# A three-stage attention and expert kernel on one TensorE: the middle experts' last two forms by pairs of quarters, blocks' sums and remainders behind the additions, weight forms in other phases

## The chip, the core and the metric

The kernel runs on one core of a Trainium2 chip. The metric is device time in microseconds. Before the change it is 2186.79 us, the median of three runs (2185.93 to 2187.22). The core has a matrix engine (TensorE, PE in the profile), a vector engine (VectorE, DVE), a scalar engine (ScalarE, ACT), GpSimd (POOL) and a sync engine (SP) whose queue issues nearly all DMA transfers. Each engine works off its own list of instructions in the order in which the program gives them, and waits at an instruction until the semaphores it names are there.

## The reference

Attention over 4 batches, 8 heads, 1152 positions of width 64 (the queries pooled in pairs) gives 2304 tokens of width 512. They go through a mixture of 8 experts of which every one sees every token, and then through a soft mixture with 32 slots.

```
x = attention(q, k, v)                       # 2304 x 512
P = exp(x @ w_gate - max)                    # 8 rounds of row and column scaling
for e in range(8):
    h = maximum(x @ w1[e], 0)                # 512 x 1024
    out += P[:, e:e+1] * (h @ w2[e])         # 1024 x 512
return softmoe(out, phi, m2_w1, m2_w2)
```

The change is in the part of the experts, above all in experts 1 to 6.

## The kernel before

**Split operands.** All matrix work is done to nearly float32 precision in a faster type: an operand is held as a rounded half and the remainder. ScalarE writes the rounded half (a cast), VectorE subtracts it from the original (the remainder), and TensorE multiplies three pairs of halves into one sum. Weights go the same way, in tiles of 128 x 1024: `f_hi` is the cast (line 532), `f_lo` the remainder (line 535).

**Experts 1 to 6 by seven forms.** The first layer of an expert is not done as eight products of quarter matrices but as seven, of sums of quarters of the tokens and of the weights (the forms 11, 12, S2, S3, 22, S1, S4, numbered 0 to 6 in `PAIR`). The second layer is done in the same way by seven products (`PRODUCTS`) with weight forms 0 to 6. The sums of weights (`fsum`, line 507) are made one expert ahead on VectorE and stored to DRAM (`fstore`, line 512); later `stage_f` loads each form into one of four staging tiles, and `f_hi` and `f_lo` split it.

**Units, chunks, products.** The tokens are worked in three units per expert. `chunk(e, u, n, f)` (line 749) is form n for quarter f of the hidden half: six matmuls of 384 columns (line 763). `product(e, i, j)` (line 808) is product j of token block i: twelve matmuls of 256 columns (line 824), and then one VectorE instruction that adds the result into the accumulator (line 836). A unit has 28 chunks and 21 products (three blocks of seven), and the list says in which order they come:

- a first phase with forms 0 and 1: 8 chunks, 7 products (block 1 of the unit before),
- a middle phase with forms 2 to 4: 12 chunks, 7 products (block 2 of the unit before),
- the phase of additions, with forms 5 and 6: 8 chunks, 7 products (block 0 of this unit).

The unit's first phase accumulates in two PSUM tiles (`g`, pool of two). Form 0's sums are copied by ScalarE into four seed banks, and form 1 goes on in the same tile; the middle phase goes on in the seed banks. In the phase of additions form 5 of a quarter begins a `g` tile; VectorE adds it to a part of the hidden values (line 783, "the addition"), ScalarE applies the relu (line 769), and form 6 of the same quarter accumulates on in the same tile, so it waits for the addition; after it comes a second addition. The next quarter but one needs the tile free, so it waits for that second addition.

**What a block needs.** `second` says behind which item each step of a block is put: `h_split` (cast on ScalarE, line 734; remainder on VectorE, line 735) makes the operand of one product, and four VectorE sums (`h_sum`, line 728) come before four of them. The tiles `ho` are three, the accumulating tiles `y` two: a product waits for its remainder, and the first products of a block for the last accumulations of the block before.

**Order.** It is written out by hand. `item` appends a chunk or product to the list, `at(k, ...)` hangs a step behind item k, `run` (line 1210) reads strings of c (chunk) and p (product). In `FORMS` and `FORMS0` a row is the form's name, and the items, counted from the start of unit 2 of the expert before (or from the last block of expert 0), behind which it is staged, cast and subtracted; `jobs` place the loads of raw weight quarters and their sums, `where` the preparation of token sums in expert 0 (`prep`). Chunks of quarter 3 call `load_x(2)` (line 768): two operand tiles `xs` of five are loaded through SP's queue, behind all that was put there before.

Of the kernel before, what the change touches and what calls it, by code (L numbers as in the profile page):

```python
# [405 lines left out]
def tile_attention__moe__softmoe(ctx, tc, q, k, v, w_gate, w1, w2, phi, m2_w1, m2_w2, out):  # L406
    nc = tc.nc
    N, D = out.shape
    E = w_gate.shape[1]
# [162 lines left out]
    NU = NBLK // 3  # L572
# [622 lines left out]
    bounds, starts, base, slots = {}, {}, [], []  # L1195
# [25 lines left out]

    ZIG = lambda n: [(n, 0), (n, 1), (n + 1, 0), (n, 2), (n + 1, 1), (n, 3), (n + 1, 2), (n + 1, 3)]
    blocks = [[0, NBLK - 1, []]]
# [3 lines left out]
    for e in range(1, E - 1):  # L1227
        for u in range(NU):
            starts[e, u] = len(items)
            run(e, u, "ccppcpcpcpcpcpc", ZIG(0), todo)  # L1230
            run(e, u, "cpcpcpc" "cpccpc" "cpccpc", [(n, f) for n in (2, 3, 4) for f in range(4)], todo)
            bounds[e, u] = len(items) - 1
            new = [[e, 3 * u + i, []] for i in range(3)]
            blocks += new
            todo += new[:1]
            run(e, u, "ccpcpcpcpcpcpcp", ZIG(5), todo)
            todo += new[1:]
            plans.append((e, u, len(items) - 1))
# [6 lines left out]
    for n, (e, i, pos) in enumerate(blocks):  # L1245
        before = blocks[n - 1][2] if n else []
        if e == 0:
            b = pos[0] - 3
            second(e, i, pos, [b, b, b, b + 1, pos[0], pos[1], pos[2], pos[3], b + 1, pos[0]])
            continue  # L1250
        u, k = divmod(i, 3)
        end = bounds[e, u] + 15
        if k == 0:
            b = bounds[e, u]
            second(e, i, pos, [b - 4, b, b, b + 2, pos[0], pos[1], pos[2], pos[3], b + 3, b + 4])
        elif k == 1:
            second(e, i, pos, [end - 3, end - 1, end - 1, end, pos[0], pos[1], pos[2], pos[3], end, end + 1])
        else:
            second(e, i, pos, [before[4], before[4] + 1, before[5], before[6], pos[0], pos[1], pos[2], pos[3],
                               before[6], before[6] + 1])  # L1260

    late = dict(late=True)
    FORMS = (
# [3 lines left out]
    )  # L1267
    FORMS0 = (
# [3 lines left out]
    )  # L1272
    WS, VS = ("S3", "S1", "S2", "S4"), (3, 4, 2, 6)
    for e in range(E - 1):
        n = e + 1
        r = starts[e, 2] if e else base[8]
        if n < E - 1:
# [4 lines left out]
            if e:  # L1282
                jobs = ((starts[e, 1] - 7, starts[e, 1] - 1, 2), (starts[e, 1] + 12, starts[e, 1] + 22, 2))
            else:
                jobs = ((base[5] + 2, base[5] + 6, 2), (base[6] + 3, base[6] + 7, 2))
            for (s, d, w), raws, names, stage in zip(jobs, (W1Q, Q), (WS, VS), (stage_w, stage_v)):
# [4 lines left out]
        else:  # L1291
            at(r, (stage_p, n, 0), (stage_p, n, 4), **late)
            at(r + 14, (p_split, n, 0, "11"), **late)
            at(r + 36, (load_x7, 0), **late)
            at(r + 45, (load_x7, 1), **late)
            at(start7 + 14, (p_split, n, 4, "v0"), **late)

    where = [base[1] + 2, base[1] + 6, base[2] + 5, base[3] + 5, base[4] + 2, base[4] + 7, base[7] + 4, base[7] + 7, base[8]]
    for n, k in enumerate(where):
# [220 lines left out]
```

## Time and profile before

| | |
|---|---|
| median of three runs | 2186.79 us |
| the profiled execution | 2185.62 us, of which the span of the trace 2183.8 us |
| TensorE busy | 2070.2 us, 95% of the span; mean granted clock 0.982 |
| VectorE, ScalarE, GpSimd busy | 1440.4, 1008.6, 410.3 us |
| DMA | 367.42 MB, mean 168 GB/s |
| chain that ended last, by engine | PE 78%, DVE 11%, ACT 5%, DMA 3%, issue 2%, SP's queue 1% |

The profile is of one execution. Its time is 1.82 us above its span and 1.17 us below the median. TensorE's rows are pipelined: a row of six matmuls lasts a little longer than the distance to the next row's start. Idle time in brackets is that of the engine just before the row, with the line that released it. In what follows [rows n] are the groups of rows of the section after the next.

### The profile page before, as it was taken

The page shows a single profiled execution, that of the slowest core. Times are in us where ns is not written, and L with a number is a line of the kernel's source. Part 1 is how long each engine was busy: PE and PEld are TensorE (multiplying, and loading weights), DVE is VectorE, ACT ScalarE, POOL GpSimd, SP SyncE. Part 2 cuts the span into 40 slices and gives each one's busy share as a digit, 9 for nine tenths or more (in the row PEclk, how much of TensorE's full clock was granted, in tenths as well). Part 3 has the DMA queues.
Part 4 walks back from the last instruction along what each step waited for, and adds up shares of the span by engine and source line. Part 5 has one row for each costly group of instructions (what it writes and reads, how often), then busy time and mean ns, then how long its engine had stood idle before and what let it go on. Part 6 is the DMA issues. An engine that isn't in the chain of part 4 may idle for free.

```text
span 2183.8 us, 37987 instructions
## 1 busy us (share of the span) xinstructions
PE 2070.2 (95%) x14800; PEld 1883.5 (86%) x14800; DVE 1440.4 (66%) x2601; ACT 1008.6 (46%) x2110; POOL 410.3 (19%) x304
## 2 busy tenths in 40 slices
PE   8999999999999899989989998999999999999996
PEld 6777777778998889989989998999999999999863
DVE  6788778878677576766666667666766655644451
ACT  4666666665444534544454444445344534211232
POOL 6888888870000000000000000000000000000000
PEclk9999999999999999999999999999999999999997
DMA  7565555444365654455455445545544333577579
GB/s 181 141 142 126 136 129 127 99 123 156 136 239 200 216 190 138 152 178 175 157 172 204 136 144 179 191 141 185 186 150 144 115 105 103 182 272 249 205 242 285
DMA packets 198978, 367.42 MB, mean 168 GB/s; under 512 B 51472, under 2 KB 116304, under 8 KB 195792
## 3 DMA queue, kind: packets, MB, share of 16 engines
q1 hardware_dynamic: 196400, 363.53, 53.1%
q8 instruction: 117, 1.92, 0.4%
q10 hardware_dynamic: 2400, 1.47, 0.3%
q14 instruction: 61, 0.50, 0.1%
HBM read 276.38 MB, written 55.84 MB: 152 GB/s over the span
## 4 chain that ended last, share of the span: by engine, by line
PE 78%; DVE 11%; ACT 5%; DMA 3%; issue 2%; SPq 1%; ACTq 0%
PE y L824 23%; PE seed L763 10%; PE g L763 10%; PE o L271 6%; PE se L245 6%; PE S L216 4%; DVE ho L735 2%; DVE ht L728 2%; ACT ho L734 2%; DVE hr L783 1%; PE g L859 1%; PE g L860 1%; PE g L858 1%; PE y L881 1%; PE y L882 1%
## 5 line engine op out<-in xcount | busy, mean ns | idle before, releaser
L824 PE MATMUL y<-v,ho 128*128 128x256 f32 x5292 | 707.4, 285 | 20.3 <-DVE acc L836 14.0
L824 PEld LDWEIGHTS y<-v,ho 128*128 128x128 f32 x5292 | 687.4, 192 | 28.1 <-DVE acc L836 12.7
L763 PE MATMUL g<-xs,w 128*128 128x384 f32 x1728 | 354.8, 344 | 54.7 <-DVE hr L783 54.7
L763 PEld LDWEIGHTS g<-xs,w 128*128 128x128 f32 x1728 | 298.9, 193 | 63.8 <-DVE hr L783 63.0
L836 DVE SCALAR_TENSOR_TENSOR acc<-y,P,acc 128x256 f32<-128x256 f32 x378 | 182.1, 482 | 218.3 <-PE y L824 217.2
L256 POOL TENSOR_TENSOR acc<-acc,e 128x576 f32<-128x576 f32 x218 | 310.6, 1425 | 28.8 <-ACT e L248 15.1
L217 DVE TENSOR_REDUCE m<-S 128x1 f32<-128x384 f32 x432 | 227.8, 554 | 74.2 <-PE S L216 58.2
L985 POOL MEMSET HT<- 128x1024 f32 x2 | 1.9, 958 | 1406.1 <-PE y L824 1406.1
L735 DVE TENSOR_TENSOR ho<-hr,ho 128x512 fp32r<-128x512 f32 x252 | 174.0, 691 | 134.8 <-ACT ho L734 130.9
L248 ACT ACTIVATE e<-se 128x288 f32<-128x288 f32 x576 | 213.3, 411 | 95.2 <-PE se L245 94.2
L763 PE MATMUL seed<-xs,w 128*128 128x384 f32 x1296 | 249.3, 337 | 2.7 <-DMA xs<-xd0T 2.7
L763 PEld LDWEIGHTS seed<-xs,w 128*128 128x128 f32 x1296 | 222.6, 190 | 3.0 <-DMA xs<-xd0T 3.0
L734 ACT CAST ho<-hr 128x512 fp32r<-128x512 f32 x252 | 155.3, 617 | 103.8 <-PE y L824 95.6
L769 ACT ACTIVATE hr<-hr 128x384 f32<-128x384 f32 x144 | 75.0, 525 | 225.7 <-DVE hr L783 225.6
L734 ACT CAST ho<-ht 128x512 fp32r<-128x512 f32 x189 | 114.4, 619 | 130.5 <-PE y L824 73.3
L245 PE MATMUL se<-q,kd 128*128 128x288 f32 x576 | 166.6, 298 | 0.8 <-DVE kp L160 0.5
L245 PE MATMUL se<-qm,kd 128*128 128x288 f32 x576 | 164.7, 295 | 0.0
L735 DVE TENSOR_TENSOR ho<-ht,ho 128x512 fp32r<-128x512 f32 x189 | 129.6, 689 | 50.2 <-ACT ho L734 49.7
L271 PE MATMUL o<-e,vr 128*64 128x288 f32 x1152 | 160.9, 415 | 0.0
L216 PE MATMUL S<-kd,q 128*128 128x384 f32 x384 | 143.1, 375 | 2.3 <-DVE m L217 1.4
L271 PEld LDWEIGHTS o<-e,vr 128*64 128x64 f32 x1152 | 74.1, 136 | 50.4 <-issue 8.4
L216 PEld LDWEIGHTS S<-kd,q 128*128 128x128 f32 x384 | 72.7, 190 | 47.9 <-issue 21.3
(211 smaller groups left out, 3031.5 us busy)
## 6 DMA issues: line engine op xcount, KB each, us to landing
stg<-in_moe_w_dram SPq DMA_DIRECT2D x96, 512.0 KB, 5.9
w<-xd SPq DMA_DIRECT2D x72, 512.0 KB, 4.9
xs<-xd0T SPq DMA_DIRECT2D x48, 384.0 KB, 3.7
xs<-xd1T SPq DMA_DIRECT2D x48, 384.0 KB, 3.6
xs<-xd2T SPq DMA_DIRECT2D x48, 384.0 KB, 3.6
kd<-kp SPq DMA_DIRECT2D x31, 576.0 KB, 6.0
xs<-xd0B SPq DMA_DIRECT2D x36, 384.0 KB, 3.6
xs<-xd1B SPq DMA_DIRECT2D x36, 384.0 KB, 3.6
```

The lines of the kernel that those rows point to most:

```text
L216: nc.tensor.matmul(ps, lhsT=w, rhs=r[:, 384 * n:384 * n + 384], start=True, stop=True)
L217: nc.vector.tensor_reduce(out=M_[ph][:, x, n:n + 1], in_=ps, axis=AX.X, op=ALU.max)
L245: nc.tensor.matmul(ps, lhsT=kd[:, z, 128 * c:128 * c + 128], rhs=y[:, h, g], start=z == 0, stop=z == 1)
L248: nc.scalar.activation(out=e[:, g], in_=ps, func=AF.Exp, scale=1.0 / 16)
L256: nc.gpsimd.tensor_tensor(out=acc_[ph], in0=acc_[ph], in1=e, op=ALU.add)
L271: nc.tensor.matmul(O_[ph][64 * g:64 * g + 64, :288], lhsT=raws["v"][pi][:, h, c, :], rhs=E_[ph, c][:, g], start=c == 0, stop=c == 8,)
L734: nc.scalar.copy(o[:, 0], p)
L735: nc.vector.tensor_tensor(out=o[:, 1], in0=p, in1=o[:, 0].bitcast(F32), op=ALU.subtract)
L763: nc.tensor.matmul(ps, lhsT=w[:, a, kk, 128 * f:128 * f + 128], rhs=x[:, :, b], start=first and kk + z == 0, stop=kk == 1 and z == 2, skip ...
L769: relu = lambda o, b: nc.scalar.activation(out=o, in_=b, func=AF.Relu)
L824: nc.tensor.matmul(ps, lhsT=o[:, x, c], rhs=v[:, w, c], start=first and c + z == 0, stop=c + z == 5, skip_group_check=not first,)
L836: nc.vector.scalar_tensor_tensor(out=y, in0=ps, scalar=p, in1=y, op0=ALU.mult, op1=ALU.add)
```

## The change

The work is the same: every chunk, product, sum, split and transfer is there as often as before, and only the order changes.

```
-    ZIG = lambda n: [(n, 0), (n, 1), (n + 1, 0), (n, 2), (n + 1, 1), (n, 3), (n + 1, 2), (n + 1, 3)]
+    ORDER = lambda n: [(n + x, f + y) for f in (0, 2) for x in range(2) for y in range(2)]
...
-            run(e, u, "ccppcpcpcpcpcpc", ZIG(0), todo)
-            run(e, u, "cpcpcpc" "cpccpc" "cpccpc", [(n, f) for n in (2, 3, 4) for f in range(4)], todo)
+            run(e, u, "ccpccppccppcpcp", ORDER(0), todo)
+            run(e, u, "cpcpcpc" "cpcpcc" "cpcpcc", [(n, f) for n in (2, 3, 4) for f in range(4)], todo)
...
-            run(e, u, "ccpcpcpcpcpcpcp", ZIG(5), todo)
+            run(e, u, "pccpccpccppcpcp", ORDER(5), todo)
...
-        end = bounds[e, u] + 15
-        if k == 0:
-            b = bounds[e, u]
-            second(e, i, pos, [b - 4, b, b, b + 2, pos[0], pos[1], pos[2], pos[3], b + 3, b + 4])
-        elif k == 1:
-            second(e, i, pos, [end - 3, end - 1, end - 1, end, pos[0], pos[1], pos[2], pos[3], end, end + 1])
-        else:
-            second(e, i, pos, [before[4], before[4] + 1, before[5], before[6], pos[0], pos[1], pos[2], pos[3],
-                               before[6], before[6] + 1])
+        b, z = bounds[e, u], bounds[e, u] + 16
+        end = (e, u) == (E - 2, NU - 1)
+        second(e, i, pos, (
+            [b - 4, b, b + 1, b + 2, b + 5, b + 6, b + 7, b + 11, b + 3, b + 4],
+            [b + 12, z - 1, b + 14, z, z + 1, z + 2, z + 4, z + 5, z - 1, z + 1] if end else
+            [b + 12, b + 15, b + 14, b + 17, b + 19, b + 21, b + 22, b + 26, b + 16, b + 18],
+            [z + 6, z + 5, z + 7, z + 8, z + 9, z + 10, z + 12, z + 13, z + 6, z + 8] if end else
+            [z + 12, z + 10, z + 13, z + 14, z + 17, z + 19, z + 21, z + 24, z + 11, z + 16],
+        )[k])
...
-        (5, 72, 80, 82), (6, 74, 83, 85),
+        (5, 73, 79, 80), (6, 75, 82, 92),
...
-                jobs = ((starts[e, 1] - 7, starts[e, 1] - 1, 2), (starts[e, 1] + 12, starts[e, 1] + 22, 2))
+                jobs = ((starts[e, 1] - 3, starts[e, 1] + 1, 2), (starts[e, 1] + 12, starts[e, 1] + 20, 2))
...
-    where = [base[1] + 2, base[1] + 6, base[2] + 5, base[3] + 5, base[4] + 2, base[4] + 7, base[7] + 4, base[7] + 7, base[8]]
+    where = [base[1 + n // 2] + (2, 7)[n % 2] for n in range(9)]
```

The ten numbers given to `second` are the places of split 0, of the two sums s1 and s2, of splits 1 to 6, and of the sums s3 and s4. b is the last item of the middle phase, z the first of the next unit. All rows of `FORMS` and `FORMS0` get new places, of which one row is shown.

The first piece is TensorE's list in the phase of additions of unit 0 of expert 3, before: `g_13279`, `g_13290`, `g_13347` and `g_13404` are the tiles of quarters 0 to 3, `w_12788` is form 5, `w_12857` form 6; a chunk is two rows, and a `y` row is a product.

```order
L763 MATMUL g_13279<-xs_13126,w_12788 128x384 x3
L763 MATMUL g_13279<-xs_13198,w_12788 128x384 x3
L763 MATMUL g_13290<-xs_13126,w_12788 128x384 x3
L763 MATMUL g_13290<-xs_13198,w_12788 128x384 x3
L824 MATMUL y_13302<-v_13090,ho_13227 128x256 x12
L763 MATMUL g_13279<-xs_13200,w_12857 128x384 x3
L763 MATMUL g_13279<-xs_13266,w_12857 128x384 x3
L824 MATMUL y_13330<-v_13116,ho_13271 128x256 x12
L763 MATMUL g_13347<-xs_13126,w_12788 128x384 x3
L763 MATMUL g_13347<-xs_13198,w_12788 128x384 x3
```

And the same place now, where the quarters' tiles are `g_13295`, `g_13307`, `g_13370` and `g_13379`.

```order
L824 MATMUL y_13278<-v_13087,ho_13228 128x256 x12
L763 MATMUL g_13295<-xs_13123,w_12886 128x384 x3
L763 MATMUL g_13295<-xs_13199,w_12886 128x384 x3
L763 MATMUL g_13307<-xs_13123,w_12886 128x384 x3
L763 MATMUL g_13307<-xs_13199,w_12886 128x384 x3
L824 MATMUL y_13317<-v_13113,ho_13292 128x256 x12
L763 MATMUL g_13295<-xs_13201,w_12944 128x384 x3
L763 MATMUL g_13295<-xs_13267,w_12944 128x384 x3
L763 MATMUL g_13307<-xs_13201,w_12944 128x384 x3
L763 MATMUL g_13307<-xs_13267,w_12944 128x384 x3
L824 MATMUL y_13278<-v_13140,ho_13304 128x256 x12
L763 MATMUL g_13370<-xs_13123,w_12886 128x384 x3
```

A product now stands ahead of the first pair, form 6 of a quarter has one chunk and one product between it and form 5, and a new quarter begins one chunk and one product behind the form 6 that it waits for, where it was one product.

The second piece is VectorE's list at the same place, before: lines 728 are the block's sums, 735 remainders, 783 additions, 836 accumulations, and the two lines 535 are the remainders of weight forms 5 and 6 for the next block.

```order
L728 TENSOR_TENSOR ht_13276<-ht_13274,hr_12900 128x512
L535 TENSOR_TENSOR v_13245<-stg_13158,v_13245 128x1024
L783 TENSOR_TENSOR hr_13137<-g_13279,hr_13137 128x384
L783 TENSOR_TENSOR hr_13137<-g_13290,hr_13137 128x384
L735 TENSOR_TENSOR ho_13299<-ht_13276,ho_13299 128x512
L836 SCALAR_TENSOR_TENSOR acc0_9067<-y_13302,P_79,acc0_9067 128x256
L735 TENSOR_TENSOR ho_13316<-ht_13274,ho_13316 128x512
L728 TENSOR_TENSOR hr_12900<-hr_12900 128x4x128
L535 TENSOR_TENSOR v_13288<-stg_13177,v_13288 128x1024
L783 TENSOR_TENSOR hr_13045<-g_13279,hr_13045 128x384
```

And now, from the same product's accumulation on.

```order
L836 SCALAR_TENSOR_TENSOR acc0_9067<-y_13278,P_79,acc0_9067 128x256
L735 TENSOR_TENSOR ho_13292<-hr_13212,ho_13292 128x512
L783 TENSOR_TENSOR hr_13138<-g_13295,hr_13138 128x384
L735 TENSOR_TENSOR ho_13304<-ht_13274,ho_13304 128x512
L783 TENSOR_TENSOR hr_13138<-g_13307,hr_13138 128x384
L728 TENSOR_TENSOR hr_12874<-hr_12874 128x4x128
L836 SCALAR_TENSOR_TENSOR acc0_9067<-y_13317,P_79,acc0_9067 128x256
L728 TENSOR_TENSOR ht_13274<-hr_13212,ht_13274 128x512
L783 TENSOR_TENSOR hr_13044<-g_13295,hr_13044 128x384
L735 TENSOR_TENSOR ho_13340<-ht_13272,ho_13340 128x512
L783 TENSOR_TENSOR hr_13044<-g_13307,hr_13044 128x384
```

Both weight remainders have left this stretch (form 6's stands behind the fourth product's accumulation), and each remainder or sum stands behind an addition.

The third piece is SP's queue where unit 0 of expert 2 goes over into unit 1, before: lines 666 load operand tiles `xs`, lines 474 the four raw quarters.

```order
L666 DMA xs_11346<-xd1B11_7182 128x768
L474 DMA stg_11474<-in_moe_w1_dram 128x2x512
L474 DMA stg_11476<-in_moe_w1_dram 128x2x512
L474 DMA stg_11478<-in_moe_w1_dram 128x2x512
L474 DMA stg_11480<-in_moe_w1_dram 128x2x512
L666 DMA xs_11489<-xd1B11_7182 128x768
L666 DMA xs_11491<-xd1B21_7187 128x768
```

And now.

```order
L666 DMA xs_11466<-xd1B21_7202 128x768
L474 DMA stg_11524<-in_moe_w1_dram 128x2x512
L474 DMA stg_11526<-in_moe_w1_dram 128x2x512
L474 DMA stg_11528<-in_moe_w1_dram 128x2x512
L474 DMA stg_11530<-in_moe_w1_dram 128x2x512
L666 DMA xs_11538<-xd1B21_7202 128x768
L666 DMA xs_11540<-xd1T2_7322 128x768
```

The four quarters have moved behind the loads that follow form 5 and stand directly ahead of those that follow form 6.

## Rows read from the trace of the kernel before

**Rows 1.** The costliest groups: count | busy us, mean ns | idle before, releaser

```profile
L824 PE MATMUL y<-v,ho 128*128 128x256 f32 x5292 | 707.4, 285 | 20.3 <-DVE acc L836 14.0 <-ACT acc L832 5.3 <-DVE v L535 0.8
...
L763 PE MATMUL g<-xs,w 128*128 128x384 f32 x1728 | 354.8, 344 | 54.7 <-DVE hr L783 54.7
```

**Rows 2.** The chain of waits, one clean stretch: start us, us, what

```profile
1115.43 2.08 PE seed L763 x12
1117.51 1.43 PE y L824 x12
```

**Rows 3.** TensorE in time order: start us, us, engine, line, tiles, [idle before, releaser]

```profile
700.46 1.23 PE L763 MATMUL g<-xs,w 128*128 128x384 f32 x6
...
740.80 1.61 PE L763 MATMUL g<-xs,w 128*128 128x384 f32 x6 [0.53 <-DVE hr L783]
...
1135.42 1.33 PE L763 MATMUL g<-xs,w 128*128 128x384 f32 x6 [1.39 <-DVE hr L783]
...
1141.77 2.29 PE L763 MATMUL g<-xs,w 128*128 128x384 f32 x6 [3.60 <-DVE hr L783]
...
1164.99 1.70 PE L824 MATMUL y<-v,ho 128*128 128x256 f32 x12 [1.84 <-DVE acc L836]
...
1203.90 1.33 PE L763 MATMUL g<-xs,w 128*128 128x384 f32 x6 [0.25 <-DVE hr L783]
...
1208.23 1.31 PE L763 MATMUL g<-xs,w 128*128 128x384 f32 x6 [1.57 <-DVE hr L783]
...
1265.50 1.31 PE L763 MATMUL g<-xs,w 128*128 128x384 f32 x6 [0.25 <-DVE hr L783]
...
1269.82 1.31 PE L763 MATMUL g<-xs,w 128*128 128x384 f32 x6 [1.59 <-DVE hr L783]
...
1329.82 1.33 PE L763 MATMUL g<-xs,w 128*128 128x384 f32 x6 [1.39 <-DVE hr L783]
...
1843.99 1.31 PE L763 MATMUL g<-xs,w 128*128 128x384 f32 x6 [0.25 <-DVE hr L783]
```

**Rows 4.** ScalarE and VectorE at the start of a phase of additions, beside TensorE

```profile
1261.58 2.24 PE L763 MATMUL g<-xs,w 128*128 128x384 f32 x12
...
1261.78 0.49 ACT L769 ACTIVATE hr<-seed 128x384 f32<-128x384 f32 x1 [1.69 <-PE seed L763]
...
1262.30 0.62 ACT L734 CAST ho<-hr 128x512 fp32r<-128x512 f32 x1
...
1267.01 0.69 DVE L735 TENSOR_TENSOR ho<-ht,ho 128x512 fp32r<-128x512 f32 x1 [1.10 <-ACT ho L734]
...
1267.62 0.48 DVE L836 SCALAR_TENSOR_TENSOR acc<-y,P,acc 128x256 f32<-128x256 f32 x1
1268.01 0.68 DVE L735 TENSOR_TENSOR ho<-ht,ho 128x512 fp32r<-128x512 f32 x1
1268.61 0.68 DVE L728 TENSOR_TENSOR hr<-hr 128x512 f32<-128x512 f32 x1
1269.21 0.55 DVE L783 TENSOR_TENSOR hr<-g,hr 128x384 f32<-128x384 f32 x1
```

**Rows 5.** A weight form's remainder on VectorE in a phase of additions

```profile
1140.03 1.22 DVE L535 TENSOR_TENSOR v<-stg,v 128x1024 fp32r<-128x1024 f32 x1
```

**Rows 6.** Two windows: busy times of five engines, granted clock, DMA share, GB/s

```profile
1132.00:1134.00 2.00, 2.00 (x16) 1.83 (x14) 1.97 (x4) 0.00 (x0) 0.00 (x0) 1.00 1.03 390
...
1142.00:1144.00 2.00, 2.00 (x7) 2.00 (x8) 1.41 (x3) 0.79 (x2) 0.00 (x0) 0.50 0.73 210
```

**Rows 7.** TensorE's wait for an operand load in expert 1

```profile
731.27 5.50 PE L763 MATMUL seed<-xs,w 128*128 128x384 f32 x21 [2.67 <-DMA xs<-xd0T]
```

**Rows 8.** TensorE's wait in the last block of expert 0

```profile
676.00 2.93 PE L824 MATMUL y<-v,ho 128*128 128x256 f32 x12 [5.31 <-ACT acc L832]
```

**Rows 9.** Costliest groups: ScalarE's rounding of token sums in expert 0

```profile
L648 ACT CAST xt<-xs 128x512 fp32r<-128x512 f32 x18 | 11.2, 620 | 27.6 <-DVE xs L643 16.5 <-DMA xd2T<-xt 8.7 <-DVE w L535 2.4
```

**Rows 10.** SP's DMA queue where four weight quarters are loaded

```profile
1130.97 10.71 SPq L474 DMA_DIRECT2D stg<-in_moe_w_dram  x4
```

More of the change, by code (lines that the diff above doesn't have):

```diff
@@ L1245, in tile_attention__moe__softmoe @@
     for n, (e, i, pos) in enumerate(blocks):
-        before = blocks[n - 1][2] if n else []
         if e == 0:
@@ L1282, in tile_attention__moe__softmoe @@
             if e:
-                jobs = ((starts[e, 1] - 7, starts[e, 1] - 1, 2), (starts[e, 1] + 12, starts[e, 1] + 22, 2))
+                jobs = ((starts[e, 1] - 3, starts[e, 1] + 1, 2), (starts[e, 1] + 12, starts[e, 1] + 20, 2))
             else:
-                jobs = ((base[5] + 2, base[5] + 6, 2), (base[6] + 3, base[6] + 7, 2))
+                jobs = ((base[5] + 6, base[5] + 10, 2), (base[6] + 6, base[6] + 10, 2))
             for (s, d, w), raws, names, stage in zip(jobs, (W1Q, Q), (WS, VS), (stage_w, stage_v)):
@@ L1292, in tile_attention__moe__softmoe @@
             at(r, (stage_p, n, 0), (stage_p, n, 4), **late)
-            at(r + 14, (p_split, n, 0, "11"), **late)
+            at(r + 18, (p_split, n, 0, "11"), **late)
             at(r + 36, (load_x7, 0), **late)
```

10 rows, old and new, of tables (FORMS, FORMS0) are left out of this document.

## The prediction

> **What bounds the kernel now.** I read the shares of the engines first: TensorE is busy 95% of the span, so a change of order can give back only the rest, and what hangs on the clock. The costliest groups with their idle time come next [rows 1]: the chunks of line 763 waited 54.7 us for additions of line 783, the products of line 824 waited 20.3 us, of it 14.0 for VectorE's accumulations and 5.3 for one of ScalarE's. Then the chain of waits gives the clean pace, two chunks in 2.08 us and a product in 1.43 [rows 2]. A unit is 28 chunks and 21 products: 28 x 1.04 + 21 x 1.43 = 59.15 us. Last, TensorE in time order around the first form-6 chunk of each unit, a marker that recurs once a unit [rows 3]; the reader should see the stall before the marker in each unit, and compare distances of markers with 59.15.
>
> From 740.80 to 1843.99, 17 units, there are 1103.2 us instead of 17 x 59.15 = 1005.6: 97.6 lost. A unit without weight work, 1203.90 to 1265.50, takes 61.60, 2.45 too much; idle are 1.57 and 0.25, so each of two stalls costs 0.3 more than its idle time (the row before it runs out, two chunks taking 2.24 where starts are 2.08 apart [rows 2, 4], and the first chunk behind a stall has 1.31 or 1.33 against 1.23). An expert, 1135.42 to 1329.82, takes 194.4 instead of 177.5. Most of that is in its first unit: 3.60 idle before 1141.77, where a weight form's remainder of 1.22 [rows 5] stands ahead of the addition on VectorE, and 1.84 before a product at 1164.99. Behind the long stall the granted clock is 0.50, 1.2 of 2.4 GHz, after 1.00 ten microseconds earlier [rows 6], and the chunk there takes 2.29.
>
> The first unit, from 700.46 to 740.80, has 22 chunks and 8 products before its marker, 34.3 us, and took 40.3: 6.0 too much, 2.67 of them a wait for an operand load [rows 7]. The last unit has one more stall behind its marker, taken as 1.57 + 0.3 = 1.9. The middle experts thus lose 97.6 + 6.0 + 1.9 = 105.5. In expert 0 one product waits 5.31 for ScalarE and then lasts 2.93 instead of some 1.6 [rows 8]: with 0.3 that is 6.9. ScalarE was held there by its rounding of token sums, which waited 8.7 in all for earlier tiles to be stored [rows 9]. In sum 112.4 us could go.
>
> **The change part by part.** No instruction is added or removed, so nothing is charged for work. What counts is how much waiting stays.
>
> *The phase of additions.* Before, form 6 of quarter 0 had one product between it and form 5 of quarter 1, and the third quarter one product behind the form 6 whose tile it takes. Now a chunk and a product lie in each place. I set the new order against the clean pace, T being the start of the phase's first product: product 0 to 1.43, chunks (5,0), (5,1) to 3.51, product to 4.94, (6,0), (6,1) to 7.02, product to 8.45, (5,2) to 9.49, (5,3). On the other engines durations are from [rows 4], each instruction starting some 0.08 before the one ahead is over: relu 0.49, cast 0.62, remainder 0.68 (spacing 0.60), sum 0.68 (0.60), accumulation 0.48 (0.39), addition 0.55.
> - The relu of the middle phase starts 0.2 behind the next item's start, as 1261.78 stands to 1261.58. Cast of split 1 to 1.35, sums meanwhile to 2.1, the first accumulation, remainder 1 to 3.13: product 1 needs it at 3.51, 0.4 to spare.
> - Addition (5,0) 3.04 to 3.59, its relu to 4.14, cast 2 to 4.67, remainder 2 to 5.39, addition (5,1) 5.30 to 5.85; (6,1) wants it at 5.98, 0.1 to spare.
> - Sum, accumulation, sum; addition (6,0) 7.36 to 7.91, in time for (5,2) at 8.45. Its relu to 8.45, cast 3 to 8.98, remainder 3 9.01 to 9.70, and only behind it addition (6,1), 9.61 to 10.16. (5,3) takes that tile and wants it at 9.49. At 1269.82 a chunk started 0.06 after its addition's end, so it starts at 10.22: 0.72 late, with 0.12 for the slower first chunk 0.84.
> - From here each addition has at least 0.8 to spare, and the next unit's first product 0.3.
>
> So 0.84 a unit is left, 18 x 0.84 = 15.1. The price is from both sides: the 0.1 and 0.4 may fail as well, and the nearest row for a failing schedule is the cheapest unit of before, 2.45; or the 0.72 vanishes if ScalarE is quicker by one round. So 0 to 2.45, 0 to 44 over all units. I take the hand schedule, nearer to zero, since one wait and not two stands in it.
>
> *Weight forms.* Form 5's remainder leaves the phase; form 6's, 1.22 and a spacing of 1.14, now stands behind the fourth product's accumulation, in the first unit of an expert. There it puts the last remainder and the next unit's first accumulations back; of 1.14 some 0.7 is slack, so about 0.45 + 0.12 = 0.58 is left, 6 x 0.58 = 3.5 (0 if the slack is larger, 6 x 1.22 = 7.3 if there is none). The stall of 3.60, and with it the low clock of 1142 to 1144, goes: nothing of that length is left in which TensorE has nothing to do. The other forms go into the middle phase, where a unit's 12 chunks and 7 products leave VectorE with sums, remainders and accumulations and no additions.
>
> *Blocks 1 and 2.* Their sums and remainders now stand an item or two ahead of their products instead of in a row; the 1.84 before 1164.99 goes. In the middle phase the first remainder of a block is due within 0.1 of its product; I leave that at nothing, and it is in the range of the phase of additions.
>
> *SP's queue.* Four loads of raw quarters held SP for 10.71 us [rows 10], since each waits for a staging tile. They stood ahead of the loads behind form 5 and stand now ahead of those behind form 6. Staging tiles come free at about T + 11.6 to 15.4, the operand loads are called at T + 18 and used near T + 23. Four quarters are 2.1 MB; DMA moved 390 GB/s in a full window [rows 6], so 5.4 us. That ends before T + 23, and I leave 1 us in all. From the other side: all of 5.4 late at five transitions between experts, 27. Between 0 and 27 I take the value near zero, as the operand wait of before occurs once [rows 7].
>
> The Trainium skill, "DMA: Bandwidth & Descriptors", section "Anatomy of one DMA — SWDGE (gpsimd) path", says that a DMA's semaphore wait happens on the issuing sequencer before dispatch. The trace agrees as to SP: 10.71 us for four issues [rows 10]. By that rule a staging tile that comes free late delays every operand load behind it; by the row's times it does not reach the loads here. The rule gives the second rival below.
>
> *Expert 0 and the first unit.* Token sums are spread evenly over blocks 1 to 5, so ScalarE's rounding no longer waits in the last blocks: the 6.9 goes, but raw quarters now start behind the stores of token sums, and a form's sum may come later; I leave 1.5 (between 0 and 6.9). In the first unit I leave 1.9 of the 6.0 (three start-up matmuls of the seeds are in it; between 0 and 6.0).
>
> *Sum.* Left are 15.1 + 3.5 + 1.0 + 1.5 + 1.9 = 23.0, gone 112.4 - 23.0 = 89.4. The profiled execution took 2185.62, 1.82 of it outside the span of 2183.8, and was 1.17 below the median: 2185.62 - 89.4 + 1.17 = 2097.4, rounded 2097.
>
> **The rivals.** *Operand loads late.* Quarters wait for staging tiles, operand loads behind them: 5 x 5.4 = 27 instead of 1, 2123. For it speaks that SP was held 10.71 us and that an operand wait of 2.67 exists; against it that the quarters are called some 6 us ahead of the loads.
>
> *Additions stay exposed.* In each unit two stalls as in before's cheapest: 18 x 2.45 = 44 instead of 18.6, 2097 + 25.5 = 2122. For it: two places have 0.1 to spare or less by my schedule. Against it: what made the 1.57 was a tile wanted one product behind its form 6, now a chunk later.
>
> *Round trips on the path (the other side).* Remainders now stand between additions, and each waits for a relu, then a cast. At 1267.01 VectorE stood 1.10 for a cast [rows 4]. If each of five such trips in a phase reaches TensorE, 5 x (1.10 + 0.3) = 7.0 a unit, 126 instead of 18.6: 2097 + 107 = 2204, slower. It turns against the change once a unit loses more than 1.03 + 89.4 / 18 = 6.0. For it: the two engines are in series in five places of the new list. Against it: four of the five have a chunk and a product beside them, 2.47 us. The Trainium skill, "PSUM — Partial Sum Buffer", section "Engine vs sequencer instructions", says that ScalarE's and VectorE's queues are strictly first in, first out, so an early wait holds all behind it. The trace agrees at 1267.01, where 1.10 us of VectorE pass idle [rows 4].
>
> *The waits only move.* Every wait taken away returns elsewhere: 2187. Nothing in the profile demands it.
>
> **How the numbers follow.** Forecast 0.71 (2097); late loads 0.10 (2123); exposed additions 0.12 (2122); waits only move 0.03 (2187); round trips 0.04 (2204). The likeliest's own range is 2085 (if 12 of the 15.1 left in the phase of additions go too) to 2112 (a second wait of 0.84 in each unit, 15). The range that holds 8 in 10 goes to the loss of both middle rivals with some of the other terms: 2084 to 2132. A measurement of this kernel can tell 0.2%, 4.4 us, from no change. Faster by more than that 0.93, within it 0.03, slower 0.04.
>
> **What the profile after would show.** Right: the chunks of line 763 wait some 15 us and no longer 54.7 for line 783, one wait of about 0.7 before the chunk (5,3) of each unit; markers 60 us apart; no granted clock of 0.50 in the middle; the 5.31 before expert 0's last block gone; no wait on operand loads in the middle. Loads wrong: waits of several us of line 763 on `xs` behind the second unit's start. Additions wrong: two or more waits on line 783 in each unit. Round trips: products of line 824 idle for remainders of line 735. What would make the forecast wrong as a whole: a middle unit that stays above 61.6.

## The result, and the profile after

The changed kernel took 2100.47 us (median of four runs, 2096.87 to 2101.21), against 2186.92 for the kernel before (four runs). The ratio is 0.9602, with a 95% interval of 0.9586 to 0.9619. The forecast was 2097, range 2084 to 2132.

The profiled execution took 2101.21, with a span of 2099.0. In the groups by cost (columns as in [rows 1]) the waits of chunks for additions have fallen from 54.7 to 9.4, those of products from 20.3 to 6.1, and the operand wait [rows 7] is gone:

```profile
L824 PE MATMUL y<-v,ho 128*128 128x256 f32 x5292 | 691.9, 282 | 6.1 <-DVE ho L735 3.4 <-ACT acc L832 1.0 <-DVE acc L836 0.9
L763 PE MATMUL g<-xs,w 128*128 128x384 f32 x1728 | 337.2, 337 | 10.5 <-DVE hr L783 9.4 <-ACT seed L771 0.8 <-DMA xs<-xd1B 0.3
...
L763 PE MATMUL seed<-xs,w 128*128 128x384 f32 x1296 | 247.6, 335 | 0.0
```

To see where the time came from, cut TensorE's time at three starts: the first row of line 794 (expert 0 begins), of line 763 (expert 1), of line 858 (expert 7). First the kernel before, in time order, whose row of line 763 at 700.46 is in [rows 3]:

```profile
483.97 0.28 PE L794 MATMUL g<-xs,w 128*128 128x256 f32 x1
...
1860.80 0.28 PE L858 MATMUL g<-w 128*128 128x256 f32 x1
```

And the changed kernel:

```profile
485.63 0.28 PE L794 MATMUL g<-xs,w 128*128 128x256 f32 x1
...
699.55 1.23 PE L763 MATMUL g<-xs,w 128*128 128x384 f32 x6
...
1775.76 0.28 PE L858 MATMUL g<-w 128*128 128x256 f32 x1
```

Cut in the same way, all profiles give this table (us; what follows expert 1 to 6 is expert 7 and the soft mixture):

| kernel | attention | expert 0 | experts 1 to 6 | what follows | span | median |
|---|---|---|---|---|---|---|
| before | 483.97 | 216.49 | 1160.34 | 323.0 | 2183.8 | 2186.92 |
| changed | 485.63 | 213.92 | 1076.21 | 323.2 | 2099.0 | 2100.47 |
| changed, once more | 483.08 | 214.18 | 1075.96 | 323.1 | 2096.3 | 2098.57 |
| remainder 3 moved | 482.90 | 213.59 | 1062.12 | 323.2 | 2081.8 | 2085.04 |
| raw quarters of expert 0 moved | 483.49 | 210.01 | 1076.99 | 323.8 | 2094.3 | 2093.75 |
| both | 483.05 | 209.87 | 1060.60 | 322.6 | 2076.1 | 2079.25 |
| old order of additions | 483.19 | 214.22 | 1127.43 | 323.5 | 2148.3 | 2149.10 |
| new order alone | 483.38 | 216.44 | 1126.42 | 322.6 | 2148.8 | 2150.51 |
| old places of sums and remainders | 484.49 | 214.36 | 1103.57 | 322.9 | 2125.3 | 2127.04 |
| old weight forms | 483.11 | 215.42 | 1093.31 | 322.9 | 2114.7 | 2115.93 |
| old expert 0 | 482.84 | 216.62 | 1083.35 | 322.5 | 2105.3 | 2107.55 |
| old raw loads | 483.49 | 214.36 | 1080.54 | 323.2 | 2101.6 | 2103.01 |

Experts 1 to 6 gave 84.1 us, expert 0 gave 2.6; attention, whose code is the same, took 1.7 more in this execution and 0.9 less in the next. The stretch of experts 1 to 6 as one window of each profile, before and then now (the stretch and its length, busy us of TensorE, of its weight loads, of VectorE, ScalarE and GpSimd, granted clock, DMA share, GB/s):

```profile
700.46:1860.80 1160.34, 1089.29 (x7481) 1076.83 (x7479) 761.32 (x1236) 538.52 (x965) 0.00 (x0) 0.98 0.48 159
699.55:1775.76 1076.21, 1064.80 (x7481) 1055.90 (x7479) 747.89 (x1236) 526.87 (x964) 0.00 (x0) 1.00 0.52 172
```

TensorE's idle time there fell from 71.0 to 11.4, which is 59.6 of the 84.1. The other 24.5 is its busy time, with the same matmuls: rows that stretch around a wait, and rows under a lower clock. In windows of 2 us the granted clock is below 0.97 in 29 of them before and in none now.

A middle unit now has one wait on TensorE, before the chunk (5,3), and the same one each time. These are TensorE's rows of the changed kernel with idle time over 0.15 between 900 and 1300 (those between that are like the others are left out; columns as in [rows 3]):

```profile
938.11 1.83 PE L763 MATMUL g<-xs,w 128*128 128x384 f32 x9 [0.25 <-DMA xs<-xd1B]
...
1105.49 1.31 PE L763 MATMUL g<-xs,w 128*128 128x384 f32 x6 [0.51 <-DVE hr L783]
1165.67 1.32 PE L763 MATMUL g<-xs,w 128*128 128x384 f32 x6 [0.51 <-DVE hr L783]
...
1285.88 1.32 PE L763 MATMUL g<-xs,w 128*128 128x384 f32 x6 [0.51 <-DVE hr L783]
```

The distance is 60.10 us, against 61.60 in before's cheapest unit and the forecast's 59.15 without waits. From the first to the second unit of an expert it is longer: 60.18 in expert 3 (1105.49 to 1165.67), 60.17 and 60.13 in experts 4 and 5, but 60.63 in expert 2, with the wait of 0.25 for operands in it, and 60.78 in expert 1, with a wait of 0.45 for an accumulation. The wait of 0.51 before 1285.88 followed back, ScalarE:

```profile
1283.60 0.52 ACT L769 ACTIVATE hr<-hr 128x384 f32<-128x384 f32 x1 [1.53 <-DVE hr L783]
1284.04 0.60 ACT L734 CAST ho<-ht 128x512 fp32r<-128x512 f32 x1
```

VectorE in the same stretch:

```profile
1283.02 0.55 DVE L783 TENSOR_TENSOR hr<-g,hr 128x384 f32<-128x384 f32 x1
1284.67 0.69 DVE L735 TENSOR_TENSOR ho<-ht,ho 128x512 fp32r<-128x512 f32 x1 [1.10 <-ACT ho L734]
1285.28 0.55 DVE L783 TENSOR_TENSOR hr<-g,hr 128x384 f32<-128x384 f32 x1
```

The addition of (6,0) at 1283.02 releases a relu, the relu is ahead of the cast of split 3, the cast releases the remainder at 1284.67, and only behind that stands the addition of (6,1), 1285.28. It ends at 1285.83, and the chunk starts at 1285.88. VectorE itself was idle for 1.10 us ahead of that.

In expert 0 the 5.31 of [rows 8] is gone, but four smaller waits are there. TensorE:

```profile
618.98 1.70 PE L824 MATMUL y<-v,ho 128*128 128x256 f32 x12 [0.98 <-ACT acc L832]
...
637.67 1.46 PE L824 MATMUL y<-v,ho 128*128 128x256 f32 x10 [1.92 <-DVE ho L735]
...
660.79 1.45 PE L824 MATMUL y<-v,ho 128*128 128x256 f32 x10 [0.94 <-DVE ho L735]
665.70 3.11 PE L824 MATMUL y<-v,ho 128*128 128x256 f32 x24 [0.46 <-DVE acc L836]
```

VectorE ahead of the 1.92 stood at the sum of a weight form (line 507) that waited for a raw quarter, with the block's remainders behind it:

```profile
635.78 1.22 DVE L507 TENSOR_TENSOR stg<-stg 128x1024 f32<-128x1024 f32 x1 [2.91 <-DMA stg<-in_moe_w_dram]
636.93 1.29 DVE L735 TENSOR_TENSOR ho<-ht,ho 128x512 fp32r<-128x512 f32 x2
```

And SP's queue, where the raw quarters (line 474) stand behind stores of token sums and of operands:

```profile
603.24 18.77 SPq L651 DMA_DIRECT2D xd2T<-xt  x8
622.06 0.63 SPq L614 DMA_DIRECT2D xd<-w  x1
622.74 5.50 SPq L624 DMA_DIRECT2D xd2B<-w  x8
628.28 2.01 SPq L474 DMA_DIRECT2D stg<-in_moe_w_dram  x4
```

### The profile page after: what moved, and what is told of

Its sections match the earlier page's. It is cut to its first block, busy times and chain, and to the rows that moved or that the text cites. A ratio compares the mean times of both kernels' runs of the same rounds, so it can differ in the third digit from the quotient of the medians.

```text
span 2099.0 us, 38009 instructions
## 1 busy us (share of the span) xinstructions
PE 2046.2 (97%) x14800; PEld 1861.9 (89%) x14800; DVE 1426.4 (68%) x2601; ACT 997.5 (48%) x2110; POOL 410.4 (20%) x304
## 3 DMA queue, kind: packets, MB, share of 16 engines
q8 instruction: 117, 1.92, 0.4%
## 4 chain that ended last, share of the span: by engine, by line
PE 80%; DVE 9%; ACT 4%; DMA 3%; issue 2%; SPq 1%; POOL 0%; ACTq 0%; DVEq 0%; POOLq 0%
PE y L824 24%; PE seed L763 10%; PE g L763 9%; PE o L271 7%; PE se L245 7%; PE S L216 4%; DVE ht L728 2%; DVE hr L783 2%; PE g L859 2%; PE g L860 2%; PE g L858 2%; PE y L881 1%; PE y L882 1%; PE y L883 1%; ACT hr L769 1%
## 5 line engine op out<-in xcount | busy, mean ns | idle before, releaser
L824 PE MATMUL y<-v,ho 128*128 128x256 f32 x5292 | 691.9, 282 | 6.1 <-DVE ho L735 3.4
L824 PEld LDWEIGHTS y<-v,ho 128*128 128x128 f32 x5292 | 673.7, 190 | 11.6 <-issue 4.7
L763 PE MATMUL g<-xs,w 128*128 128x384 f32 x1728 | 337.2, 337 | 10.5 <-DVE hr L783 9.4
L763 PEld LDWEIGHTS g<-xs,w 128*128 128x128 f32 x1728 | 292.3, 189 | 19.0 <-DVE hr L783 15.5
L778 ACT COPY hr<-seed 128x384 f32<-128x384 f32 x144 | 69.2, 480 | 127.9 <-PE seed L763 127.4
```

The lines of the kernel that those rows point to most:

```text
L763: nc.tensor.matmul(ps, lhsT=w[:, a, kk, 128 * f:128 * f + 128], rhs=x[:, :, b], start=first and kk + z == 0, stop=kk == 1 and z == 2, skip ...
L824: nc.tensor.matmul(ps, lhsT=o[:, x, c], rhs=v[:, w, c], start=first and c + z == 0, stop=c + z == 5, skip_group_check=not first,)
```

## The experiments

All are compared with the kernel before on the same chip; for the size of an effect the table's columns are used, since attention moves by up to 2.8 us from run to run. The medians of the table come from four sets of runs, in which the kernel before took 2186.92, 2183.05, 2182.80 and 2183.80; the changed kernel was in the first two of them.

**The changed kernel once more.**

> The changed kernel once more, as the yardstick for the others on the same chip. Theory (the middle is regular, what varies from run to run lies ahead of the experts): 2100.5 within 2, and the distance of the markers, the form-6 or form-5 chunks that wait for line 783, stays 60.10 within 0.05. Rival (the middle varies): markers move by some tenths from unit to unit.

2098.57 us, ratio 0.9614 (0.9601 to 0.9627). From the second unit on the markers stand 60.08 to 60.21 apart, and 60.76 behind the first, so the theory's 0.05 does not hold for the first unit of an expert. Experts 1 to 6 take 1075.96, 0.25 less than the first time, and the wait for operands in expert 2 is not there: the middle is regular up to such tenths, and what varies more lies ahead of it.

**Remainder 3 behind the second addition.**

```diff
-            [b - 4, b, b + 1, b + 2, b + 5, b + 6, b + 7, b + 11, b + 3, b + 4],
+            [b - 4, b, b + 1, b + 2, b + 6, b + 6, b + 7, b + 11, b + 3, b + 4],
```

> One number moved: the remainder of split 3 stands behind the second addition of form 6 and no longer ahead of it. Theory: this remainder, which waits for a relu and a cast, is what holds addition (6,1) and so the chunk (5,3), 0.51 idle and some 0.3 of restart in each unit; gone, 18 x 0.8 = 14 us less than the changed kernel, 2086, units of 59.3. Rival 1: the wait moves to the product that needs this remainder, units stay at 60.1, 2100. Rival 2: the addition is late because of ScalarE's relu of (6,0), which is not moved: 2100 and the wait still names line 783.

2085.04 us, ratio 0.9550 (0.9537 to 0.9563). Experts 1 to 6 took 1062.12, 14.0 less than the mean of the two profiles of the changed kernel. TensorE at the place of the wait, chunks (5,2) and (5,3) now in one row, two in 2.09:

```profile
1272.25 1.59 PE L824 MATMUL y<-v,ho 128*128 128x256 f32 x12
1273.68 2.25 PE L763 MATMUL g<-xs,w 128*128 128x384 f32 x12
1275.77 3.03 PE L824 MATMUL y<-v,ho 128*128 128x256 f32 x24
...
1335.07 3.03 PE L824 MATMUL y<-v,ho 128*128 128x256 f32 x24
```

The wait did not move to the product that needs the remainder (both rows of products run without idle time). The last two rows are the same place in two units that follow each other, 59.30 apart. So the wait cost 60.10 - 59.30 = 0.80 a unit, and its cause is shown: the remainder's place in VectorE's list, not ScalarE's relu, which was not moved. The 0.15 by which 59.30 is above 59.15 is not the wait's.

**Raw quarters of expert 0.**

```diff
-                jobs = ((base[5] + 6, base[5] + 10, 2), (base[6] + 6, base[6] + 10, 2))
+                jobs = ((base[5] + 4, base[5] + 10, 2), (base[6] + 6, base[6] + 12, 2))
```

> In expert 0 the four raw quarters of the first layer are called two items earlier, ahead of the operand stores of block 6, and the sums of those of the second layer two items later. Theory: the three waits of products for remainders and accumulations in expert 0 (1.92, 0.94 and 0.46 at 637.67, 660.79 and 665.70) come from VectorE standing at a weight sum whose raw quarters had not landed (2.91 and 0.79 idle); they shrink, 2 to 4 us less than the changed kernel, 2097 to 2098. Rival: the quarters wait for staging tiles, not behind the stores: 2100.

2093.75 us, ratio 0.9593 (0.9580 to 0.9606). Expert 0 took 210.01, 4.0 less, at the upper end of what was expected; of its waits only the first, for ScalarE's accumulation, is left, and VectorE's waits of 2.91 and 0.79 for raw quarters are gone. The quarters now go ahead of the nine stores of operands (lines 614 and 624), but still behind the eight stores of token sums (line 651), which take 19.05 of SP's queue. The median is 4.8 below the changed kernel's on this chip. Which of the two places gave how much was not tried apart.

**Both.** The two edits above in one kernel.

> The two edits together (remainder 3 behind the second addition, raw quarters of expert 0 as in the run before this). Theory: they lie in different stages and add up, 14 + 3 = 17 less than the changed kernel, 2083 to 2084. Rival: one of the two gives nothing, 2086 or 2097.

2079.25 us, ratio 0.9524 (0.9511 to 0.9537): 19.3 below the changed kernel on this chip. The parts, 13.5 and 4.8 in the medians, add up to 18.3; the theory had put expert 0's part at 3, and its time is some 4 above the measured one. This version beats both kernels.

**The old order in the phase of additions**, all else new.

```diff
-            run(e, u, "pccpccpccppcpcp", ORDER(5), todo)
+            run(e, u, "ccpcpcpcpcpcpcp", ZIG(5), todo)
```

> The changed kernel, but the phase of additions in the order of before (quarters in zigzag, one product between the two forms of a quarter); sums, remainders and weight forms stay in their new places. Theory: the order of the chunks is what spares the additions; the cheapest unit of before lost 2.45 and one of the changed kernel 0.95, so at least 18 x 1.5 = 27 comes back, 2126, more (to 2150) where new remainders stand ahead of additions with little room. Rival (the places of sums and remainders carried the gain): within 5 of the changed kernel, 2100.

2149.10 us, ratio 0.9845 (0.9830 to 0.9859): experts 1 to 6 51 more than in the changed kernel, the upper end. In every unit but the first TensorE waits 2.04, longer than before's 1.57 in a plain unit, one without weight work [rows 3], since the new place of the remainder meets an order without room. Besides, at the start of the second unit of experts 1 to 5 a chunk waits 0.99 to 1.40 for operand tiles, 6.2 us in all, which neither theory nor rival had. TensorE, such a wait of 2.04 and then one for operands:

```profile
1115.88 1.58 PE L824 MATMUL y<-v,ho 128*128 128x256 f32 x12
1119.50 1.31 PE L763 MATMUL g<-xs,w 128*128 128x384 f32 x6 [2.04 <-DVE hr L783]
...
1137.84 1.83 PE L763 MATMUL g<-xs,w 128*128 128x384 f32 x9 [1.08 <-DMA xs<-xd1B]
```

VectorE, where behind the remainder an accumulation and a sum too come ahead of the addition at 1118.90:

```profile
1117.30 0.69 DVE L735 TENSOR_TENSOR ho<-ht,ho 128x512 fp32r<-128x512 f32 x1 [1.10 <-ACT ho L734]
1117.90 0.48 DVE L836 SCALAR_TENSOR_TENSOR acc<-y,P,acc 128x256 f32<-128x256 f32 x1
1118.30 0.68 DVE L728 TENSOR_TENSOR hr<-hr 128x512 f32<-128x512 f32 x1
1118.90 0.55 DVE L783 TENSOR_TENSOR hr<-g,hr 128x384 f32<-128x384 f32 x1
```

**The new order alone**, on the kernel before.

```diff
-            run(e, u, "ccppcpcpcpcpcpc", ZIG(0), todo)
-            run(e, u, "cpcpcpc" "cpccpc" "cpccpc", [(n, f) for n in (2, 3, 4) for f in range(4)], todo)
+            run(e, u, "ccpccppccppcpcp", ORDER(0), todo)
+            run(e, u, "cpcpcpc" "cpcpcc" "cpcpcc", [(n, f) for n in (2, 3, 4) for f in range(4)], todo)
...
-            run(e, u, "ccpcpcpcpcpcpcp", ZIG(5), todo)
+            run(e, u, "pccpccpccppcpcp", ORDER(5), todo)
```

> The kernel before, with TensorE's new order of chunks and products alone; sums, remainders, weight forms and expert 0 as before. Theory: the waits behind VectorE's additions in plain units go (27), those from weight forms and from rows of sums and remainders stay in part: 2140 to 2160. Rival 1 (the order is everything): 2105, expert 0's 3 left out. Rival 2 (the order alone is worth nothing, as the old remainders now stand in new places ahead of additions): 2175 or more.

2150.51 us, ratio 0.9850 (0.9835 to 0.9864): 33.9 of the 84.1 us in experts 1 to 6. The number is the theory's, and both rivals fall, but the theory's mechanism does not hold. The waits of plain units have not gone, they stand at other chunks. TensorE, the second form-6 chunk of two units and a chunk between:

```profile
1186.66 1.32 PE L763 MATMUL g<-xs,w 128*128 128x384 f32 x6 [0.93 <-DVE hr L783]
1189.78 2.35 PE L763 MATMUL g<-xs,w 128*128 128x384 f32 x12 [0.36 <-DVE hr L783]
...
1248.22 1.33 PE L763 MATMUL g<-xs,w 128*128 128x384 f32 x6 [0.94 <-DVE hr L783]
```

From the first of these rows to the last are 61.56 us, against before's 61.60. What the order alone gave lies where weight forms are: from the phase of additions of unit 0 to that of unit 1 of expert 4 it takes 65.4, where before's marker distance was 68.5, and from unit 2 of expert 3 to unit 0 of expert 4 61.7, where it was 64.3. The longest wait for an addition there is 1.06 and no longer 3.60.

**The old places of sums and remainders**, with the new order, weight forms and expert 0. The three rules that the diff removes stand again in place of the lists; one line of it:

```diff
-            [b - 4, b, b + 1, b + 2, b + 5, b + 6, b + 7, b + 11, b + 3, b + 4],
+            second(e, i, pos, [b - 4, b, b, b + 2, pos[0], pos[1], pos[2], pos[3], b + 3, b + 4])
```

> The changed kernel, but sums and remainders of each block by the rules of before; TensorE's order, weight forms and expert 0 stay new. If the parts add up, the order alone (middle experts 1126.4 us) less the weight forms (17.2 in the run that put them back) less expert 0's part in the first unit (7.1) leaves 1102, 26 more than the changed kernel's 1076.2: 2126. Theory: additions again stand behind sums and remainders, two or more waits for line 783 in each plain unit, 20 to 30 more. Rival (with the new order the places of sums and remainders hardly matter, and order plus forms explain all): within 5 of the changed kernel, 2100 to 2105.

2127.04 us, ratio 0.9740 (0.9724 to 0.9756). Experts 1 to 6 took 1103.57; 1102 had been worked out from three other runs. There are two waits in a plain unit again, which takes 61.59. TensorE:

```profile
1172.53 1.31 PE L763 MATMUL g<-xs,w 128*128 128x384 f32 x6 [0.94 <-DVE hr L783]
1175.66 2.35 PE L763 MATMUL g<-xs,w 128*128 128x384 f32 x12 [0.39 <-DVE hr L783]
```

**The old weight forms**, the table `FORMS` of before for experts 2 to 6.

```diff
-        (5, 73, 79, 80), (6, 75, 82, 92),
+        (5, 72, 80, 82), (6, 74, 83, 85),
```

(one line of it; the whole table goes back.)

> The changed kernel, but the weight forms of experts 2 to 6 staged, cast and subtracted where they were before. Theory: a form's remainder of 1.22 in the phase of additions, where the schedule has 0.1 to 0.8 of room, stops TensorE again, in the first unit of five experts and with the low clock behind it: of the 17 that an expert of before lost, some 9.6 are not the plain units' 3 x 2.45; I expect 3 to 10 an expert, 2115 to 2150. Rival (the new order has room enough): within 3 of the changed kernel.

2115.93 us, ratio 0.9690 (0.9674 to 0.9706), at the low end of the theory: 17.2 in experts 1 to 6, 3.4 for each of five experts. Markers put 1.1 of the 3.4 in the third unit of the expert before and 2.3 in the first unit, where the theory had it all. In both a form's remainder stands again between two additions. VectorE, third and first unit:

```profile
1047.42 1.22 DVE L535 TENSOR_TENSOR w<-stg,w 128x1024 fp32r<-128x1024 f32 x1
...
1106.53 1.22 DVE L535 TENSOR_TENSOR v<-stg,v 128x1024 fp32r<-128x1024 f32 x1
...
1108.67 0.55 DVE L783 TENSOR_TENSOR hr<-g,hr 128x384 f32<-128x384 f32 x1
```

And TensorE, which in the third unit waits 1.67 where it was 0.51, and in the first for that addition and for the next:

```profile
1049.16 1.33 PE L763 MATMUL g<-xs,w 128*128 128x384 f32 x6 [1.67 <-DVE hr L783]
...
1109.27 1.31 PE L763 MATMUL g<-xs,w 128*128 128x384 f32 x6 [0.44 <-DVE hr L783]
1111.53 1.31 PE L763 MATMUL g<-xs,w 128*128 128x384 f32 x6 [0.95 <-DVE hr L783]
```

The granted clock stays at 1.00 there, so the low clock of [rows 6], which I had expected back, is no part of the 17.2.

**The old expert 0**: `FORMS0`, `where` and the raw loads of expert 0 as before.

```diff
-    where = [base[1 + n // 2] + (2, 7)[n % 2] for n in range(9)]
+    where = [base[1] + 2, base[1] + 6, base[2] + 5, base[3] + 5, base[4] + 2, base[4] + 7, base[7] + 4, base[7] + 7, base[8]]
```

(`FORMS0` and one line of `jobs` go back too.)

> The changed kernel, but token sums, raw quarters and weight forms in expert 0 as before. Theory: the 5.31 wait for ScalarE's accumulation in the last block comes back and the three smaller waits go; the stage of expert 0 was 216.5 us before and 213.9 in the changed kernel, so 2.6 more, 2103. Rival (the prediction's term): 5.4 more, 2106.

2107.55 us, ratio 0.9654 (0.9640 to 0.9668): 7 more than the changed kernel's first median, which is from another set of runs, and above both numbers. Expert 0 took 2.6 more, as the theory said, but both theories had left out what is behind it: 7.3 in experts 1 to 6, in their first unit. TensorE there:

```profile
730.44 5.45 PE L763 MATMUL seed<-xs,w 128*128 128x384 f32 x21 [2.74 <-DMA xs<-xd0T]
...
743.06 1.33 PE L763 MATMUL g<-xs,w 128*128 128x384 f32 x6 [0.94 <-DVE hr L783]
...
749.65 1.31 PE L763 MATMUL g<-xs,w 128*128 128x384 f32 x6 [2.08 <-DVE hr L783]
```

The operand wait of [rows 7] is back, and so are waits for additions: remainders of weight forms (line 535) start on VectorE at 739.06, just ahead of the first addition, and at 743.53 and 747.91, between additions; in the changed kernel none stands between the first addition and the chunk (5,3).

**The old raw loads** in experts 1 to 5.

```diff
-                jobs = ((starts[e, 1] - 3, starts[e, 1] + 1, 2), (starts[e, 1] + 12, starts[e, 1] + 20, 2))
+                jobs = ((starts[e, 1] - 7, starts[e, 1] - 1, 2), (starts[e, 1] + 12, starts[e, 1] + 22, 2))
```

> The changed kernel, but in experts 1 to 5 the raw quarters for the next expert are called four items earlier, ahead of the operand loads behind form 5, and the sums two items earlier or later, as before. Theory: the four quarters still find staging tiles when the operand loads are not yet due, so between 0 and 2 us an expert, 2100 to 2108. Rival (the prediction's second rival): operand loads stand 5.4 us behind the quarters at five transitions, 27 more, 2127, with waits of line 763 for operand tiles.

2103.01 us, ratio 0.9633 (0.9619 to 0.9648). The rival falls: chunks of experts 1 to 6 wait 0.7 us for operand tiles in all. The 4.5 in experts 1 to 6 are mostly of another kind, which neither theory named: VectorE's sums of weight forms come two items earlier, ahead of accumulations that products wait for. Such waits grew from 0.45 to 3.56. Loads and sums were not moved back apart. TensorE in the second unit of experts 1 and 3 (in 4 and 5 as in 3):

```profile
760.18 1.67 PE L824 MATMUL y<-v,ho 128*128 128x256 f32 x12 [1.60 <-DVE acc L836]
...
1122.53 1.67 PE L824 MATMUL y<-v,ho 128*128 128x256 f32 x12 [0.65 <-DVE acc L836]
```

## Why the prediction was right, point by point

**The whole.** The case given 0.71 came, 3.5 us above its number, which is inside its own range of 2085 to 2112. On the profiled execution 2096.2 was forecast and 2101.21 measured, 5.0 more: 1.7 in attention, which is the same code, 2.8 in expert 0, 0.2 in what follows, 0.4 outside the span; experts 1 to 6 took some 0.1 less than forecast.

**Experts 1 to 6.** Forecast were 105.5 lost before and 21.5 left; without waits they would take 1160.34 - 105.5 = 1054.8, so 21.4 are left. That they agree so well is in part luck: the terms are off by a few us each, in both directions. *The phase of additions* was right in place and order: one wait, before (5,3), caused by the remainder that I had named, and its removal took the wait away. Its price, 0.84, is near the 0.80 that the removal gave, but by two errors that offset each other: idle was 0.51 where I had 0.72, and around it 0.29 is lost where I had 0.12 ((5,2) to (5,3) is 1.71 and (5,3) to the next product 1.17, each instead of 1.04). My 59.15 for a unit without waits was 0.15 too low, as 59.30 with the remainder moved shows: 18 x 0.15 = 2.7 of the 105.5 could not go. *The weight form's* 0.58 in the first unit measured 0.03 to 0.08 in experts 3 to 5; why is not shown, but it fits more slack than the 0.7 that I set against its 1.14. *SP's queue* left a wait of 0.25 in one profile and none in the next, where I had 1. The T + 11.6 to 15.4 for its raw quarters stood there without rows; in the unit with T = 1275.65 SP was held by them from 1287.65 for 3.85, T + 12.0 to 15.9. The wait of 0.45 in expert 1, behind a sum of weight forms, I had not named. *The first unit* left more than 1.9: from 699.55 to its chunk (5,3) at 743.69 lie 25 chunks and 10 products, 40.3 us, and it took 44.1, of which 0.7 is the unit's own wait, so 3.1. *The clock* I had not priced apart; it is in the distances that I summed, and as forecast no granted clock of 0.50 is left there.

**Expert 0** is the term that was most mis-sized. I left 1.5 of 6.9; 216.49 - 213.92 = 2.6 went and 4.3 stayed. The mechanism was named (raw quarters behind the stores of token sums, a form's sum late), but not that VectorE would stand at that sum with the block's remainders behind it. Moving the raw quarters ahead, with later sums of the second layer, gave 4.0 back. On the other hand the same edits are worth 7.3 in the first unit, where I had credited 4.1: 9.8 measured for this piece against 9.5 in the sum.

**The rivals.** *Operand loads late* was wrong for this kernel: its own chunks wait 0.25 for operand tiles. It is no empty rival, though: with the old order of additions, and the raw loads in their new places, its sign is there, waits of line 763 on `xs` in the second unit of five experts, but at some 1.2 each and not 5.4. *Additions exposed*: one wait a unit, not two; with the old places of sums and remainders it would have been right (two waits a unit, 27.5 us more in experts 1 to 6, where I had priced it at 25.5). *Round trips*: VectorE does stand 1.10 us for a cast several times in each phase of additions, as at 1284.67, but only one of them reached TensorE; the others have a chunk and a product beside them. *The waits only move* did not happen.

**How the parts combine.** Undone one at a time, they cost in expert 0 and experts 1 to 6 together 51.5 (order of additions), 27.8 (sums and remainders), 18.6 (weight forms, of which 1.4 in expert 0, that the edit does not touch), 9.8 (expert 0), 4.8 (raw loads): 112.5, where all together gave 86.7. They do not add up: an order with room for additions is of use when nothing long stands ahead of them, and the other way round. A plain unit shows it best. It takes 61.60 before, 61.6 with the new order and the old places of sums and remainders, 62.1 to 63.1 with the old order and the new places, and 60.10 with both. The new order alone gave 34, none of it in plain units. Why undoing the order costs more than that is seen in the rows of that run: the new remainders, without the room, make a wait of 2.04 where before's was 1.57, operand tiles come late, and behind some of the waits the granted clock falls, so that of its 51 us in experts 1 to 6 idle time is 35.7 and longer rows are 15.7. One more place moved with the change, a split of expert 7's operands (`p_split`); no run undid it apart, and what follows expert 6 stays within 322.5 to 323.8 in all of them.

## What to carry to other kernels

When two engines that work in series (here relu and cast on one, addition and remainder on the other) feed a third, write the third's list so that between an item and the one that needs its result there is enough unrelated work to cover the feeders' chain, and in the feeders' lists put what the third waits for ahead of what has a later due time. Here one product, 1.43 us, was too little; a chunk and a product, 2.47 us, were enough in all places but one. Both lists have to change together: either one alone gained nothing in a plain unit. A schedule made by hand from start distances in the trace found the one wait that was left, and its removal was one number. A sum that waits for a load does harm through what is queued behind it: look whether its load can be issued ahead of stores in the same queue.

## What was unexpected of the hardware

The same idle time of TensorE is followed by different clocks. In the run with the old order of additions, waits of 2.04 us stand before chunks at 804.40 and at 1119.50 (the latter row is shown with that run). The columns of the windows are those of [rows 6]:

```profile
804.40 2.25 PE L763 MATMUL g<-xs,w 128*128 128x384 f32 x6 [2.04 <-DVE hr L783]
...
804.00:806.00 2.00, 1.60 (x5) 1.60 (x6) 1.90 (x4) 1.03 (x2) 0.00 (x0) 0.62 0.00 0
806.00:808.00 2.00, 2.00 (x11) 2.00 (x10) 0.69 (x2) 0.72 (x2) 0.00 (x0) 0.53 0.00 0
...
1119.00:1121.00 2.00, 1.50 (x9) 1.50 (x10) 1.89 (x4) 1.04 (x2) 0.00 (x0) 1.00 0.00 0
```

Behind the first the granted clock fell to 0.62 and then 0.53, nearly the lower level of 1.2 GHz, and the chunk lasted 2.25; behind the second it stayed at 1.00, 2.4 GHz, and the chunk lasted 1.31. Of the 17 waits of 2.04 in that run, 8 were followed by such a fall. With the new order alone it fell to 0.52 at 1312, behind two waits of 0.95 and 0.94 that are one chunk apart; the same pair of waits at 1498.59 was not followed by a fall. No run here tells what decides. In the changed kernel, whose longest wait in experts 1 to 6 is 0.77, it did not fall there.
